# Pooled attention with a rotated token and channel mix: another order of the hand-written table from its 701st piece on

## The chip, the cores and the metric

The kernel runs on one core of a Trainium2 chip. The metric is the device time of one execution in microseconds. TensorE (PE) multiplies matrices; VectorE (DVE), ScalarE (ACT) and GpSimd (POOL) do the elementwise work; SyncE (SP) issues DMAs.

## What is computed

For 8 batches, 8 heads, 576 positions and a head width of 64, in fp32 (q, k and two of the weights are scaled up by 8 in the inputs):

```python
k_p = k.reshape(B, H, Sp, pool, D).mean(axis=3)      # pool = 8, so Sp = 72
v_p = v.reshape(B, H, Sp, pool, D).mean(axis=3)
scores = scale * np.matmul(q, k_p.transpose(0, 1, 3, 2))
attn = softmax(scores)                               # max taken off, sum + 1e-9
x = heads_side_by_side(np.matmul(attn, v_p))         # [8, 576, 512]
theta = x @ w_theta
zr, zi = x * np.cos(theta), x * np.sin(theta)
y = einsum('ts,bsd->btd', w_tok_r, zr) + einsum('ts,bsd->btd', w_tok_i, zi)
u = x + y
out = u + np.maximum(u @ w_ch, 0.0)
```

## The kernel before

The large products are made of three matmuls each: both factors are split into a high part in the matmul's own type (fp32r) and the rest, and high times high, high times low and low times high are added in PSUM. So every elementwise result that feeds TensorE costs a cast and a subtraction more.

The work is cut into streams, one for each step of each batch, and each stream into pieces of one to a few instructions. A stream is a Python generator; each `yield` ends a piece. The letters, with the helper and the lines of its instructions:

- k, v, u: loads of keys and values (L539 kpst, L552 kprst, L542 vpst, L555 vprst). Q: loads of queries, eight DMAs (L634 qsst), and their transpose on DVE (L639 qT). K, V: pooling by halving additions (L191), and the pooled keys' way to PE (L611, L621).
- S, soften: scores (L732), maximum (L774), L792, exponent (L797), sum (L799), reciprocal (L801), normalising (L804), and a DVE transpose into the one buffer G (L819).
- E, turn: eight DMAs of each piece carry G into eraw (L863), of which there is one buffer. X, attend: the products with the pooled values (L885, L894, tiles pv) and the copies into xa and xb, the two halves of x, two buffers each. The copies of batch b + 2 go into the buffers of batch b.
- Y and y: x goes out to memory (L917 xs, L924 hall) and back turned (L932 xt).
- T, rotate: x @ w_theta (casts xe, xh, xl; L947 pt, one PSUM bank), the range reduction (L951 on ACT, L953 on DVE), sine and cosine (L707, L961, L963) and z (L1005, L1007; the last chunk of 64 positions through L994, L1020 and L1022).
- Z, take: the split of z for the mix, zh (L206 on ACT, L208 on DVE or POOL, 128x1152) and zl (L1038 on DVE, L191 on POOL). M, mix: three times nine matmuls (L1053, tiles py), the addition into xa or xb (L1059), and the split of u (uh, and L1066 or L191 ul).
- F, final: three times four matmuls (L1081, tiles pf), `u + max(pf, 0)` (L1086), a DVE transpose into R (L1092, two buffers for all batches but the last) and four DMAs to the output (L1097).

A name like F1.3.0 is batch 1, channel chunk 3, half 0 of the positions (half 0: 256 of them, xa; half 1: 320, xb); T2.4 is batch 2, position chunk 4.

The order is the table SCHEDULE, 2,131 words written out by hand. Each word takes one stream one piece further, and a last letter a, v or g puts the elementwise work of that piece on ACT, DVE or POOL:

```python
for word in SCHEDULE.split():
    name, engine = (word[:-1], word[-1]) if word[-1] in "vga" else (word, None)
    now[0] = engine
    next(streams[name])
```

Instructions stand on each engine in the order in which the table makes them, and each engine works its row in order. All DMAs behind the preparation go through SP's queue but half of those of batch 7's output, which go through ACT's. On POOL an operation on 512 or more columns is cut in two. The next transpose into a buffer of R has to wait until the four DMAs that read it have landed.

Of the kernel before, what the change touches and what calls it, by code (L numbers as in the profile page):

```python
# [1221 lines left out]
```

## Time and profile before

| | |
|---|---|
| median of 3 runs | 589.93 us (589.21, 589.93, 592.08) |
| the profiled execution | 588.76 us, span 587.0 us |
| mean granted clock of TensorE | 0.984 |
| busy: PE, DVE, ACT, POOL | 559.7, 423.4, 307.5, 302.0 us |
| DMA | 70.63 MB, mean 120 GB/s |

The profiled execution's time is the span from the first to the last instruction and 1.8 us around it. Busy times are shares of a span in which the engines work side by side; PE's of 95% says that PE is nearly always at work, and the rest is in single gaps, so one reads what ends each gap and what stands in front of that.

### The profile page before, as it was taken

To read this page: it belongs to the slowest core of one execution; us is meant where nothing else is said; L and a number is where in the kernel's file an instruction comes from. 1 tells how busy PE (TensorE), PEld (TensorE's weight loads), DVE (VectorE), ACT (ScalarE), POOL (GpSimd) and SP (SyncE) were. 2 spreads that over 40 slices of the span, in tenths; PEclk is the share of its full clock that TensorE was granted. 3 is DMA by queue.
4 is the path that set the end of the run, shared out by engine and by line. 5 is a ranking of instruction groups with operands and counts; after the bars stand their busy time and mean duration, and the time that the engine had idled before them with its cause. 6 is when DMAs were issued, how large, how long until landed. Compare 5 with 4: busy or idle time off the path is not lost.

```text
span 587.0 us, 13259 instructions
## 1 busy us (share of the span) xinstructions
PE 559.7 (95%) x4904; PEld 502.4 (86%) x4904; DVE 423.4 (72%) x834; ACT 307.5 (52%) x628; POOL 302.0 (51%) x446
## 2 busy tenths in 40 slices
PE   8779979999999998999999989999999999999996
PEld 7566869888989878989898869899998989989996
DVE  5968997879886876577786868588777876434444
ACT  2867996668635862177527644286422745144100
POOL 1423432348785676664865664483576555352220
PEclk9988979999999998999999999999999999999999
DMA  9985412678375665594555754684445441230215
GB/s 276 273 261 114 121 51 79 114 129 131 80 140 133 151 130 132 120 180 127 108 131 139 152 121 119 132 182 103 94 92 145 116 80 49 55 88 9 41 26 89
DMA packets 191265, 70.63 MB, mean 120 GB/s; under 512 B 149600, under 2 KB 176224, under 8 KB 191200
## 3 DMA queue, kind: packets, MB, share of 16 engines
q1 hardware_dynamic: 186336, 69.18, 53.2%
q10 hardware_dynamic: 4864, 0.59, 0.7%
q8 instruction: 39, 0.64, 0.5%
q14 instruction: 26, 0.21, 0.1%
HBM read 45.15 MB, written 15.73 MB: 104 GB/s over the span
## 4 chain that ended last, share of the span: by engine, by line
PE 72%; DMA 10%; SPq 6%; DVE 5%; ACT 2%; POOL 1%; issue 1%; DVEq 0%; ACTq 0%; POOLq 0%
PE py L1053 36%; PE pt L947 14%; PE pf L1081 11%; SPq L863 2%; PE s L732 2%; DMA z<-in_v_dram 2%; SPq L1097 2%; DMA out_dram<-R 1%; DMA xt<-hall 1%; DMA wraw<-in_moe_w_tok_r_dram 1%; PE pv_av L894 1%; DMA kpst<-in_k_dram 1%; PE pv_av L885 1%; DMA qsst<-in_q_dram 1%; SPq L634 1%
## 5 line engine op out<-in xcount | busy, mean ns | idle before, releaser
L1053 PE MATMUL py<-WTh,zh 128*128 128x256 f32 (+1 forms) x576 | 87.6, 299 | 3.3 <-ACT zh L206 1.3
L1053 PE MATMUL py<-WTl,zh 128*128 128x256 f32 (+1 forms) x576 | 88.4, 298 | 0.0
L1053 PE MATMUL py<-WTh,zl 128*128 128x320 f32 (+1 forms) x576 | 86.8, 297 | 0.0
L1053 PEld LDWEIGHTS py<-WTh,zh 128*128 128x128 f32 x576 | 80.5, 190 | 7.1 <-issue 2.1
L191 POOL TENSOR_TENSOR en<-e_eps,ri 128x256 f32<-128x256 f32 (+3 forms) x74 | 44.3, 616 | 78.6 <-DVE ri L801 48.6
L1053 PEld LDWEIGHTS py<-WTh,zl 128*128 128x128 f32 x576 | 79.6, 189 | 3.0 <-issue 1.3
L1053 PEld LDWEIGHTS py<-WTl,zh 128*128 128x128 f32 x576 | 81.5, 192 | 0.7 <-issue 0.4
L191 POOL TENSOR_TENSOR zl<-z,zh 128x384 fp32r<-128x384 f32 (+1 forms) x68 | 53.4, 817 | 14.1 <-ACT zh L206 9.4
L206 ACT CAST zh<-z 128x1152 fp32r<-128x1152 f32 x22 | 25.3, 1154 | 49.1 <-PE py L1053 41.6
L947 PE MATMUL pt<-th,xh 128*128 128x512 f32 x148 | 42.4, 409 | 3.5 <-ACT xh L206 1.9
L1081 PE MATMUL pf<-uh,chh 128*128 128x256 f32 (+1 forms) x256 | 44.0, 297 | 0.0
L1081 PE MATMUL pf<-uh,chl 128*128 128x256 f32 (+1 forms) x256 | 43.6, 295 | 0.0
L1081 PE MATMUL pf<-ul,chh 128*128 128x256 f32 (+1 forms) x256 | 43.3, 295 | 0.0
L797 ACT ACTIVATE e_eps<-e_eps 128x576 f32<-128x576 f32 (+1 forms) x30 | 20.3, 678 | 43.9 <-DVE e_eps L792 43.9
L947 PE MATMUL pt<-tl,xh 128*128 128x512 f32 x148 | 40.6, 397 | 0.0
L947 PE MATMUL pt<-th,xl 128*128 128x512 f32 x148 | 40.2, 394 | 0.0
L951 ACT ACTIVATE g<-pt,c_magic 128x512 f32<-128x512 f32 x35 | 24.0, 686 | 30.5 <-PE pt L947 23.6
L1081 PEld LDWEIGHTS pf<-uh,chh 128*128 128x128 f32 x256 | 37.5, 188 | 2.5 <-issue 0.5
L1081 PEld LDWEIGHTS pf<-ul,chh 128*128 128x128 f32 x256 | 37.1, 188 | 1.1 <-issue 0.5
L1081 PEld LDWEIGHTS pf<-uh,chl 128*128 128x128 f32 x256 | 37.3, 188 | 0.7
L953 DVE SCALAR_TENSOR_TENSOR g<-g,pt 128x512 f32<-128x512 f32 x35 | 23.8, 681 | 17.2 <-ACT g L951 17.0
L947 PEld LDWEIGHTS pt<-th,xh 128*128 128x128 f32 x148 | 25.9, 192 | 9.3 <-ACT xh L206 2.5
(276 smaller groups left out, 1279.1 us busy)
## 6 DMA issues: line engine op xcount, KB each, us to landing
kpst<-in_k_dram SPq DMA_DIRECT2D x15, 512.0 KB
vpst<-in_v_dram SPq DMA_DIRECT2D x28, 256.0 KB
qsst<-in_q_dram SPq DMA_DIRECT2D x96, 72.0 KB
hall<-xs SPq DMA_DIRECT2D x48, 128.0 KB
xt<-hall SPq DMA_DIRECT2D x12, 512.0 KB
eraw<-G SPq DMA_DIRECT2D x144, 40.0 KB
out_dram<-R SPq DMA_DIRECT2D x112, 40.0 KB
out_dram<-R SPq DMA_DIRECT2D x112, 32.0 KB
```

The lines of the kernel that those rows point to most:

```text
L191: nc.gpsimd.tensor_tensor(out[:, r], a[:, r], b[:, r], op)
L206: nc.scalar.copy(out, src)
L634: queue.dma_start(st[32 * i : 32 * i + 32, S * c : S * c + S].rearrange("p (x a) -> p x a", a=32), q[b, 2 * j + c + 4 * (i // 2)].rearrang ...
L732: nc.tensor.matmul(scs[hh][o : o + 64, SP * c : SP * c + SP], qT[r, c, t0 + o : t0 + o + 64], kpT[r, c, SP * hh : SP * hh + SP], start=Tru ...
L797: nc.scalar.activation(e[:n], e[:n], AF.Exp, scale=scale)
L863: queue.dma_start(Ex[32 * j : 32 * j + 32, 0:m, i], Gx[32 * i : 32 * i + 32, 0:m, j])
L947: nc.tensor.matmul(pt, l[:, c, :], r[:, c, :], start=i == 0, stop=i == 11)
L951: nc.scalar.activation(g, pt, AF.Identity, bias=c_magic)
L953: nc.vector.scalar_tensor_tensor(g, g, MAGIC, pt, ALU.subtract, ALU.subtract)
L1053: nc.tensor.matmul(py[:, :n], l[:, kk, :], r[:, kw, t], start=i == 0, stop=i == 3 * NK - 1)
L1081: nc.tensor.matmul(pv[:, :n], l[:, kk, o], uhl[r][:, kk, t], start=i == 0, stop=i == 11)
L1097: (nc.scalar if b == B - 1 and i % 2 else nc.sync if b == B - 1 else queue).dma_start(out[b, t, ch0 : ch0 + 32].rearrange("(x t) a -> t x ...
```

## The change

All pieces stay, and the first 700 words of the table are the same. From the 701st word on the order differs: a piece stands on average 4.3 places from where it stood, and some loads and poolings up to 110. 120 elementwise pieces get another engine, 44 of them in the mix. Nothing else in the file differs. PE has the same 1,035 rows of the order as before and SP the same 200, in another order; DVE gets nine instructions more, POOL four fewer, ACT 13 fewer, among them six loads of function tables. The table's rows tell a reader little; two lines of its 83:

```diff
@@ -59,83 +59,83 @@
...
-M1.0.1 Y2.0 S3.4 S3.2 T2.1g Z1.2g T2.0 T2.0 T2.0a M1.3.1 M1.0.1g S3.2 M1.0.0 S3.2g E2.2 M1.3.1 S3.2g T2.0 M1.1.1g
...
-F1.3.0 T2.4a T2.4 K4a K4.2g T2.4 F1.0.1 F1.2.0 T2.4 Z2.1a k5.0 E3.0 F1.3.0 Y3.2 K4 Z2.0g F1.1.0 F1.1.0 F1.3.0 K5.0g
...
+M1.0.1 Y2.0 S3.4 S3.2 T2.1g Z1.2g T2.0 T2.0 T2.0a M1.3.1 M1.1.0a M1.3.1 E2.2 M1.0.0 M1.3.1 M1.3.0 T2.1 S3.2 M1.1.0v
...
+k5.0 F1.1.0 T2.4a K4.2g T2.4 T2.4 F1.3.0 T2.4 K5.0g Z2.1v K4a F1.3.0 T3.3a K4 M2.1.0 E3.0 Z2.1v F1.3.0 M2.1.0 M2.1.0
...
```

What that is in instructions, at the places that the prediction speaks of. The listings give line, operation, tiles and shape; a name like R_2_0_3041 is chunk 2, half 0, and a running number. First **SP's queue where the transfers of batch 3's second attention half stand** (eraw_0), before:

```order
L863 DMA eraw_0_3049<-G 32x2x160 x8
L924 DMA hall_2_3019<-xs_2_2914 32x8x128 x2
L863 DMA eraw_0_3049<-G 32x2x160 x8
L542 DMA vpst_1_3132<-in_v_dram 64x2x512 x2
L1097 DMA out_dram<-R_1_0_3070 32x8x32 x4
L1097 DMA out_dram<-R_2_0_3041 32x8x32 x4
L555 DMA vprst_3317<-in_v_dram 64x1x512 x2
L634 DMA qsst_1_3350<-in_q_dram 32x18x32 x8
```

and in the changed kernel:

```order
L863 DMA eraw_0_3079<-G 32x2x160 x16
L542 DMA vpst_1_3166<-in_v_dram 64x2x512 x2
L1097 DMA out_dram<-R_2_0_3156 32x8x32 x4
L555 DMA vprst_3194<-in_v_dram 64x1x512 x2
L1097 DMA out_dram<-R_1_0_3154 32x8x32 x4
L634 DMA qsst_1_3317<-in_q_dram 32x18x32 x8
```

The two pieces of eraw stand side by side, and the load of vprst stands between the two groups of output.

Second, **DVE where the take of batch 2 starts** (the tile z is what the take reads, zh_1 and zl_1 its first results, R_2_0 and R_1_0 results of batch 1), before:

```order
L1020 TENSOR_TENSOR z<-px_4_2994,sn_4_2999 64x512
L1092 STREAM_TRANSPOSE R_2_0_3041<-xa_1380 128x256
L1022 TENSOR_TENSOR z<-px_4_2994,g_4_2981 64x512
L1086 SCALAR_TENSOR_TENSOR xa_1380<-pf_1_0_2988,xa_1380 128x256
L1092 STREAM_TRANSPOSE R_1_0_3070<-xa_1380 128x256
L1038 TENSOR_TENSOR zl_1_3045<-z,zh_1_3044 128x640
L1038 TENSOR_TENSOR zl_1_3045<-z,zh_1_3044 128x512
```

and in the changed kernel:

```order
L1086 SCALAR_TENSOR_TENSOR xa_1380<-pf_1_0_2989,xa_1380 128x256
L1020 TENSOR_TENSOR z<-px_4_3010,sn_4_3030 64x512
L1022 TENSOR_TENSOR z<-px_4_3010,g_4_2987 64x512
L208 CAST zh_1_3054<-z 128x1152
L1038 TENSOR_TENSOR zl_1_3055<-z,zh_1_3054 128x640
L1038 TENSOR_TENSOR zl_1_3055<-z,zh_1_3054 128x512
L1086 SCALAR_TENSOR_TENSOR xa_1380<-pf_3_0_3021,xa_1380 128x256
```

No transpose into R stands between z's parts any more (both stand some ten rows further down), and the cast zh_1, which was on ACT, stands behind z.

Third, **PE at chunk 4 of batch 4's rotation** (pt_4, ahead of the take of batch 4; the pf are final matmuls of batch 3), before:

```order
L947 MATMUL pt_3_4694<-th,xl_3_4421 128x512 x4
L1081 MATMUL pf_0_0_4716<-uh_4206,chh 128x256 x4
L1081 MATMUL pf_1_0_4728<-uh_4206,chh 128x256 x4
L1081 MATMUL pf_1_0_4728<-uh_4206,chl 128x256 x4
L1081 MATMUL pf_1_0_4728<-ul_4207,chh 128x256 x4
L947 MATMUL pt_4_4744<-th,xh_4_4725 128x512 x4
```

and in the changed kernel:

```order
L1081 MATMUL pf_0_0_4678<-uh_4167,chh 128x256 x4
L1081 MATMUL pf_1_0_4695<-uh_4167,chh 128x256 x4
L947 MATMUL pt_3_4709<-th,xh_3_4410 128x512 x4
L947 MATMUL pt_3_4709<-tl,xh_3_4410 128x512 x4
L947 MATMUL pt_3_4709<-th,xl_3_4411 128x512 x4
L1081 MATMUL pf_1_0_4695<-uh_4167,chl 128x256 x4
L1081 MATMUL pf_0_0_4678<-uh_4167,chl 128x256 x4
L1081 MATMUL pf_1_0_4695<-ul_4168,chh 128x256 x4
L947 MATMUL pt_4_4754<-th,xh_4_4732 128x512 x4
```

Two groups of pf matmuls have moved ahead of chunk 3, and five groups instead of four stand ahead of chunk 4.

## Rows read from the trace of the kernel before

**Rows 1.** The windows behind the 700th piece: busy us of each engine, then clock, DMA.

```profile
187.00:352.00 165.00, 157.79 (x1434) 138.93 (x1432) 120.48 (x233) 89.54 (x142) 108.78 (x160) 0.99 0.63 137
225.00:250.00 25.00, 23.95 (x185) 22.71 (x185) 14.27 (x28) 4.11 (x8) 15.61 (x22) 0.93 0.57 127
226.04:230.50 4.46, 4.46 (x24) 4.46 (x25) 2.09 (x4) 0.18 (x1) 0.98 (x3) 0.62 0.57 172
352.00:455.00 103.00, 101.89 (x942) 93.37 (x943) 79.54 (x153) 45.94 (x74) 60.14 (x87) 1.00 0.58 124
455.00:581.30 126.30, 126.30 (x974) 118.86 (x973) 69.22 (x143) 42.88 (x62) 48.28 (x70) 1.00 0.31 61
```

**Rows 2.** TensorE's waits from 185 to 587 us: us in total, times, longest us.

```profile
PE pt L947 <- ACT xh L206: 1.9, 3, 0.8
PE pt L947 <- DVE g L953: 1.6, 1, 1.6
PE py L1053 <- ACT zh L206: 1.3, 1, 1.3
PE py L1053 <- DVE xb L1086: 1.1, 1, 1.1
...
PE py L1053 <- DVE zh L208: 0.4, 1, 0.4
```

**Rows 3.** The chain of waits at 222 to 228 us: start, us, what.

```profile
221.94 1.73 DMA out_dram<-R
...
224.84 1.16 ACT zh L206
```

**Rows 4.** The same chain view at 341 to 361 us.

```profile
341.79 1.90 DMA eraw<-G
...
346.08 3.23 DMA out_dram<-R
...
352.20 3.01 PE pt L947 x12
```

**Rows 5.** SP's timeline, its DMA issues: start, us, engine, line, operation, count.

```profile
185.22 1.33 SPq L542 DMA_DIRECT2D vpst<-in_v_dram  x2
...
243.41 1.32 SPq L555 DMA_DIRECT2D vprst<-in_v_dram  x2
...
268.21 13.55 SPq L863 DMA_DIRECT2D eraw<-G  x16
...
337.32 5.06 SPq L863 DMA_DIRECT2D eraw<-G  x8
342.49 4.05 SPq L1097 DMA_DIRECT2D out_dram<-R  x8
```

**Rows 6.** SP's waits from 185 to 352 us, first and last of 22 groups.

```profile
SPq L1097 <- DVE ri L801: 1.7, 2, 1.5
...
SPq L924 <- DVE z L1007: 0.2, 1, 0.2
```

**Rows 7.** Groups by line and shape over the whole span: busy us, mean ns of one, idle before.

```profile
L707 ACT ACT_TABLE_LOAD x22 | 28.2, 1283 | 1.9 <-DVE g L953 1.5
...
L206 ACT CAST zh<-z 128x1152 fp32r<-128x1152 f32 x22 | 25.3, 1154 | 49.1 <-PE py L1053 41.6 <-POOL z L191 3.1 <-DVE z L1022 1.8
...
L208 DVE CAST zh<-z 128x1152 fp32r<-128x1152 f32 x4 | 3.0, 756 | 0.2
```

**Rows 8.** The chain of waits at 240 to 252 us: start, us, what.

```profile
242.92 1.65 DMA out_dram<-R
...
245.40 0.72 DVE ul L1066 x2
246.12 1.34 DVE zl L1038 x2
...
250.84 1.20 PE pt L947 x4
```

**Rows 9.** VectorE's timeline from 262 to 270 us, one row.

```profile
266.17 0.84 DVE L819 STREAM_TRANSPOSE G<-en 128x640 f32<-128x640 f32 x1
```

More of the change, by code (lines that the diff above doesn't have):

```diff
@@ L136 @@
-F7.2.1 M7.2.0 F6.2.0 F7.3.1 M7.2.0 M7.2.0v F7.2.1 F7.3.1 F7.3.1 M7.3.0g F7.2.0 M7.0.0g M7.2.0v F7.2.0 F7.3.1 F7.3.1
-F7.2.0 F7.2.0 F7.3.0 F7.3.0 F7.3.0 F7.1.0 F7.2.0 F7.2.1g F7.3.1g F7.1.0 F7.1.0 F7.3.0 F7.3.0 F7.1.0 F7.0.0 F7.0.0
-F7.0.0 F7.2.0g F7.1.0 F7.3.0g F7.0.0 F7.1.0a F7.0.0 F7.0.0a
+M1.0.1 Y2.0 S3.4 S3.2 T2.1g Z1.2g T2.0 T2.0 T2.0a M1.3.1 M1.1.0a M1.3.1 E2.2 M1.0.0 M1.3.1 M1.3.0 T2.1 S3.2 M1.1.0v
+y2.0 M1.3.1 S3.2g S3.2g M1.0.1a M1.3.0 S3.3 M1.1.1g T2.0 E2.2 S3.3 v3.1 M1.0.1v T2.0v F0.0.1 S3.3 S3.2 F0.0.1 S3.3g
@@ new lines @@
+M1.3.0 S3.3v M1.3.0 M1.3.0a V3.1g S3.4 S3.4 T2.1 M1.3.1a M1.2.1 M1.2.1 F0.2.1 S3.3 S3.4 X2.2 S3.4g Y2.2 S3.4g M1.2.1
+u3 X2.2a Y2.2 Y2.2 F0.1.1 X2.2a M1.2.1 X2.2a M1.2.0 T2.0v T2.4a S3.4 T2.1 T2.1 T2.2v M1.3.1v S3.1 S3.0 M1.2.0 T2.1
+k4.2 M1.2.1g T2.1 M1.2.0 M1.2.1v T2.2g F1.1.1 T2.1a T2.1 F1.1.1 T2.3a M1.3.0v T2.1v T2.2 M1.2.0 F0.2.1 F1.1.1 F1.3.1
+T2.2 M1.2.0a S3.0 k4.0 Y2.2 F1.3.1 S3.0 T2.1g F1.1.1 F1.3.1 S3.0 T2.2 M1.0.0a F1.2.1 T2.3g V3g S3.0g Y2.2 S3.0g F1.3.1
+F1.3.1 F1.1.1 F1.0.1 E3.2 S3.1 F1.0.1 T2.2 S3.1 y2.2 F1.0.1 T2.2 E3.2 F1.2.1 F1.0.1 F1.2.1 S3.1 K4.0g T2.2 S3.0 T2.2a
@@ new lines @@
+M2.0.1 T2.4 M2.0.0 v4.2 M2.0.1 M2.0.1 Z2.2v M2.0.0 X3.0 M2.0.1 V4.2g F1.1.0 M2.0.1v M2.0.0 M2.1.1v Z2.3a M2.1.0g V4.1v
+Z2.3v M2.0.0 F1.0.0 Y3.0 F1.3.0 M2.2.1 X3.0v X3.0a X3.0a M2.2.1 K4v Y3.0 M2.2.1 M2.0.0a Q4.1 T3.1a M2.2.1 V4g Y3.0
+M2.3.0 M2.0.0v M2.3.0 k5.2 T3.1v M2.2.1v T3.1 Q4.1 T3.1 Y3.0 M2.2.0 T3.1 S4.0 T3.0a S4.0 Y3.0 T3.1 T3.1 v4.0 S4.1
+M2.2.0 S4.0 M2.2.1g T3.1 S4.0 F1.0.0 S4.0v K5.2g M2.0.1g M2.2.0 M2.3.0 T3.1a T3.0g y3.0 M2.2.0 S4.0g M2.2.0a T3.0 T3.0
+S4.1 T3.1 S4.1 S4.0 T3.1v M2.3.0 V4.0g M2.3.0a M2.3.1 T3.0 T3.1v M2.2.0g S4.1 T3.2a M2.3.1 F1.3.0 T3.0 S4.1g M2.3.1
@@ new lines @@
+F2.0.0 M2.3.0g S4.1v T3.0 T3.0 y3.2 Q5.0 S4.1 F2.0.0 T3.0a k5.1 T3.0 M2.3.1 T3.3 T3.3 T3.0v T3.0v F2.0.0 T3.3 v5.2
+K5.1g S4.3 S4.2 T3.2v F2.0.0 F2.2.0 F2.2.0 F2.2.0 T3.3 T3.3 F2.2.0 T3.2 E4.0 M2.3.1a T3.3 T3.3a T3.2 E4.0 T3.3 S4.2
+F2.2.0 S4.2 T3.2 T3.3g M2.3.1g F2.2.1 T3.3v F2.1.1 T3.2 S4.2 F2.1.1 F2.2.1 F2.2.1 T3.2 T3.2 F2.1.1 S4.2g F2.0.0 K5
+F2.2.1 F2.3.1 F2.2.0 T3.2a S4.2g F2.1.1 F2.0.1 S4.3 T3.2 F2.3.1 F2.3.1 S4.2 T3.2g v5.1 F2.0.1 F2.0.1 F2.3.1 F2.0.0
+T3.2g Z3.0a F2.0.1 F2.2.1 S4.4 F2.2.1 S4.3 M3.0.0 F2.1.0 Q5.0 u4 K5a Z3.0g M3.0.0 S4.3 F2.1.0 F2.1.0 S4.3g F2.1.0
@@ new lines @@
+F2.3.0 M3.0.0 F2.3.0 S4.3g S4.4 Q5.1 F2.1.0 F2.3.0 S4.4 X4.0 Z3.1a S4.3 F2.1.0 F2.3.0 K5 V5.1g Z3.1g M3.0.0 S4.4
+F2.3.0 Y4.0 X4.0v Y4.0 v5.0 S4.4g M3.0.1 M3.0.1 X4.0v Y4.0 X4.0a M3.0.1 S4.4g K5a Q5.1 S4.4 F2.3.0 M3.1.1 S5.2 Y4.0
+Z3.2a S5.2 T4.0a F2.0.1 T4.1g S5.2 M3.1.1 M3.0.1 V5.2g Y4.0 E4.2 S5.2 T4.1v T4.0g T4.0 M3.1.1 T4.0 T4.0 S5.3 M3.1.0
+T4.0 y4.0 M3.1.0 Z3.3a M3.1.1 M3.1.1a F2.3.1 V5.0g Z3.2v M3.1.0 M3.0.1v S5.2v S5.2g S5.4 M3.0.0a M3.1.0 S5.3 M3.2.1
+M3.2.1 E4.2 S5.3 T4.0 Z3.3g M3.2.1 v6.1 T4.1 M3.0.1g S5.3 M3.3.0 S5.2 T4.0 S5.3g S5.3g S5.4 T4.0a T4.0 M3.3.0 M3.3.0
@@ new lines @@
+F2.0.1 F2.1.1 T4.0g S5.3 X4.2 M3.2.1 M3.3.0 Y4.2 M3.3.1 S5.4 M3.2.0 Y4.2 Y4.2 M3.1.0a S5.4 Q6.0 k6.2 M3.2.1a X4.2v
+T4.0g V6.1g S5.4g X4.2a F2.1.1 T4.1 X4.2v T4.1 T4.1 M3.1.1v Y4.2 S5.4v T4.3v T4.3g M3.2.1g T4.2a S5.4 F2.3.1 M3.2.0
+Y4.2 T4.2g S5.0 S5.0 M3.3.0g M3.2.0 T4.1 M3.2.0 M3.3.1 k6.0 M3.3.1 M3.3.1 K6.2g S5.0 S5.1 M3.3.1v M3.1.0v M3.2.0a T4.1
+F3.1.1 M3.3.0v M3.3.1v F3.3.1 F3.3.1 F3.1.1 V5v F3.1.1 T4.1a S5.0 F3.1.1 F3.3.1 S5.0v T4.2 T4.1 F3.1.1 S5.0g F3.3.1
+S5.1 E5.2 S5.1 y4.2 T4.1g T4.2 T4.2 F3.2.1 M3.2.0g F3.3.1 F3.2.1 T4.1g F3.2.1 F3.0.1 S5.1 u5 E5.2 T4.2 F3.2.1 F3.0.1
@@ new lines @@
+S6.1 S6.2 T5.0a M4.2.1 T5.3 F4.1.0 T5.2a F4.1.0 F4.1.0 T5.0 T5.0v T5.3 T5.0v M4.1.1g T5.2v F4.1.0 T5.3 M4.3.1 T5.3
+K7.0g k7.1 T5.3 F3.3.0 M4.3.1 M4.3.1 F4.1.0 S6.2 T5.3 M4.3.1 T5.3v E6.0 S6.2 T5.3 K7.1g T5.2 T5.2 K7.2g M4.2.1a S6.2
+T5.3v T5.3v T5.2 M4.3.1a M4.2.1v F4.0.0 F4.0.0 F4.0.0 F4.0.0 F4.3.1 T5.2 T5.2 M4.3.1g S6.2v T5.2 F4.3.1 T5.2a T5.2
+S6.2g F4.1.0 F4.3.1 E6.0 F4.2.1 S6.3 S6.4 F4.3.1 F4.3.1 S6.3 F4.2.1 F4.2.1 T5.2g F4.2.1 F4.0.0 Q7.0 S6.3 F4.3.0 F4.3.1
+F4.3.0 F4.3.0 T5.2g Z5.1g F4.1.1 F4.1.1 F4.1.1 Z5.0a F4.3.0 F4.2.0 F4.0.0 S6.2 Z5.0g v7.1 M5.0.0 F4.1.1 M5.0.0 M5.0.0
@@ new lines @@
+Q7.1 u6 S6.3 M5.0.1 S6.3g F4.2.1 S6.3g M5.0.0 K7 M5.0.1 K7a S6.4 Z5.1v M5.0.1 F4.2.0 K7 X6.0 F4.2.1 Z5.2g M5.1.0 S6.3
+S6.4 S6.4 S6.4g S6.4v M5.1.0 F4.3.0 X6.0a X6.0a M5.1.0 S6.4 M5.0.1 F4.3.0 M5.1.1 Y6.0 M5.1.0 Q7.1 Y6.0 Y6.0 M5.1.1 K7v
+F4.0.1 F4.0.1 Z5.2g V7.1g F4.0.1 X6.0a M5.1.1 F4.0.1 Z5.3a E6.2 F4.0.1 M5.1.1 S7.2 S7.2 E6.2 Y6.0 S7.3 M5.2.1 M5.2.1
+S7.2 Z5.3v M5.0.1a M5.2.1 F4.1.1 M5.3.1 Y6.0 F4.0.1 M5.3.1 S7.2 S7.2g S7.2v S7.3 M5.2.1 M5.1.1a X6.2 M5.3.1 M5.3.0
+S7.2 S7.3 X6.2a S7.3 X6.2v M5.1.1g X6.2a M5.3.0 Y6.2 Y6.2 Y6.2 S7.4 y6.0 M5.0.0g M5.0.1g T6.3a S7.3g T6.3v M5.3.0
@@ new lines @@
+M5.3.1 S7.3g T6.3 S7.4 Y6.2 M5.1.0g M5.3.1g S7.4 M5.3.0 S7.3 T6.3 M5.2.1g Y6.2 M5.3.1g M5.2.1g S7.4 T6.3 v7.2 F5.2.1
+F4.1.1 M5.3.0v S7.4v F5.2.1 u7 F5.2.1 S7.0 V7.2g T6.2g M5.2.0 S7.4v T6.3 T6.3 S7.4 T6.2g M5.2.0 S7.0 T6.3 F5.2.1 T6.3v
+S7.0 M5.3.0v T6.2 F5.1.1 T6.2 T6.1v y6.2 T6.2 T6.3 T6.3v T6.0a T6.3v E7.2 M5.2.0 F5.2.1 M5.2.0 T6.2 T6.2 T6.0g E7.2
+F5.1.1 F5.1.1 F5.0.1 T6.2 S7.0 F5.0.1 T6.0 T6.0 V7g F5.1.1 F5.1.1 T6.2a F5.1.1 T6.2 S7.0v T6.2v T6.0 T6.2v F5.3.1
+F5.3.1 T6.4v T6.1v F5.3.1 M5.2.0a T6.0 M5.1.0v X7.2 T6.0 F5.0.1 F5.3.1 T6.0 F5.3.1 F5.2.1 T6.0a M5.0.0g Y7.2 T6.1
@@ new lines @@
+M5.2.0g F5.0.1 T6.0 T6.1 F5.2.0 F5.0.1 X7.2a T6.1 T6.0g Y7.2 F5.2.0 X7.2a T6.0g X7.2v F5.1.0 Y7.2 F5.1.0 T6.1 Y7.2
+S7.1 F5.0.1 T6.4g F5.2.0 T6.1 T6.4a F5.1.0 T6.4v T6.1 T6.1v Y7.2 T6.4 F5.3.1 F5.1.0 T6.1 F5.2.0 T6.4 T6.4 F5.3.0
+F5.0.0 F5.3.0 T7.2g S7.0g T6.1g T6.1v F5.0.0 S7.1 T7.3a T6.4 T6.4 T7.2v T6.4 T7.3g T7.2 T6.4 y7.2 T6.4v F5.0.0 T6.4
+T7.2 F5.3.0 T7.2 T6.4 T6.4 Z6.1v F5.0.0 T6.4 S7.1 F5.3.0 F5.1.0 Z6.1g S7.1 Z6.0a M6.1.0 M6.1.0 M6.1.1 M6.1.0 T6.4 S7.0
+M6.1.0 T7.2 Z6.0g S7.1g M6.1.1 S7.1g T7.2 M6.1.1 Z6.3a S7.1 Z6.3g M6.0.1 M6.1.1 M6.0.1 F5.1.0 M6.0.1 M6.0.0 M6.0.0
@@ new lines @@
+T7.1 F6.3.0 T7.0v F6.3.0 T7.0v F6.3.0 F6.1.1 F5.2.0 T7.1 F6.1.1 T7.1 F6.3.0 F6.3.0 F6.1.1 F6.1.0 T7.1 F6.1.0 F6.3.1
+F6.1.0 F6.1.0 F6.1.0 F6.3.1 F6.3.1 F6.3.1 F6.0.0 F6.0.0 F6.2.0 T7.1a T7.1 F6.0.0 T7.1g T7.1g Z7.0v F6.3.0 F6.2.0
+F6.1.0 F6.0.0 F6.2.0 M7.0.0 Z7.0v M7.0.0 F6.2.0 F6.0.1 M7.0.1 M7.0.1 Z7.1a Z7.1v M7.0.0 M7.0.0 M7.0.1 M7.0.1 M7.1.1
+M7.1.1 M7.1.1 M7.0.1v M7.1.1 M7.1.0 F6.0.0 M7.0.0v M7.1.0 Z7.2g Z7.2g Z7.3v M7.1.1v M7.1.0 M7.2.1 Z7.3g M7.2.1 M7.2.1
+M7.1.0 M7.3.1 M7.3.1 M7.0.1g M7.3.1 F6.0.1 M7.2.1 F6.0.0 F6.1.1 M7.3.1 M7.2.1v M7.3.0 M7.3.0 M7.3.1v M7.3.0 M7.2.1v
@@ new lines @@
+M7.1.1v F6.2.1 F7.1.1 F6.1.1 F6.3.1 F7.1.1 M7.3.0 F6.2.1 M7.3.1g M7.3.0a F7.1.1 F7.1.1 M7.1.0v F7.1.1 F7.0.1 F7.0.1
+F7.0.1 M7.3.0g M7.2.0 F7.0.1 F7.0.1 F7.1.1g M7.1.0g M7.0.0g F7.2.1 F6.2.0 F7.2.1 F7.2.1 F7.0.1g M7.2.0 F7.2.1 M7.2.0
+F7.3.1 M7.2.0 M7.2.0g F7.3.1 F7.2.1 F7.3.1 F6.3.1 F7.2.0 F6.2.0 F7.2.0 M7.2.0g F7.2.1v F7.2.0 F7.3.1 F7.3.1 F7.3.0
+F7.3.0 F7.3.1a F7.3.0 F7.2.0 F7.1.0 F7.2.0 F7.3.0 F7.1.0 F7.1.0 F7.3.0 F7.0.0 F7.1.0 F7.2.0a F7.1.0 F7.3.0v F7.1.0g
+F7.0.0 F7.0.0 F7.0.0 F7.0.0 F7.0.0a
```

91 lines of the change are left out of this document (19 added, 72 removed).

## The prediction

> **What bounds the kernel now.** I read the windows first, then TensorE's waits, then the DMA queue's own timeline and waits, then the chain of waits at the two places where TensorE stood longest. The order of the two kernels is the same up to the 700th piece, at about 185 us, so only what lies behind counts. There the windows [rows 1] show three stretches. From 187 to 352 us PE is busy 157.79 of 165.00 us, so it stands for 7.2 us, and from 226.04 to 230.50 it is busy throughout but at a granted clock of 0.62, a mix of its two levels 2.4 and 1.2 GHz: at full clock that work would have taken 4.46 x 0.62 = 2.8 us, so 1.7 us are lost. From 352 to 455 us it stands for 1.1 us, from 455 to 581.3 us not at all, and the last 5.7 us are the tail behind the last matmul. All that any order of the rest can win from PE's stalls is therefore 7.2 + 1.7 + 1.1 = 10.0 us, which would put the profiled run's 588.76 us at 578.8.
>
> PE's waits [rows 2] say on whom: a cast of x (xh) on ACT, a range reduction (g) on DVE, the casts of z (zh) on ACT and DVE, an addition into xb on DVE. None is a slow engine. The chain behind the first of the two long ones [rows 3] goes back to a transfer: an out-going DMA of an earlier batch lands at 223.67, only then may DVE transpose the next result into its buffer R; the z that the take of batch 2 needs stands behind that transpose on DVE, the cast (zh, at 224.84) behind z on ACT, and the first mix matmul (226.04) behind the cast. The chain behind the other [rows 4] has the same form with a queue in front: SP's last of eight out-going issues is done at 346.08, it lands 3.23 us later, then come an R on DVE, ACT's copy of the next attention result, ACT's and DVE's g, and the rotation of chunk 4 of batch 4 (pt4_4) starts at 352.20.
>
> So the second bound is **the SP queue**. Its timeline [rows 5] reads as a belt without gaps: the eight transfers of eraw take 5.06 us to issue at 337.32, the eight out-going ones 4.05 at 342.49. From 185.22 us to the end of that last row, 346.54, the order lists 253 issues on SP, in the kernel before and in the changed one, of the same kinds in the same numbers: 161.3 us / 253 = 0.64 us each. SP's own waits for somebody else in that stretch [rows 6] are 22 groups, from 1.7 us down to 0.2 each, 11.6 us in all. Whatever PE wins, a gate that opens with the 253rd issue comes earlier only as far as those 11.6 us shrink.
>
> Here a rule speaks against this reading. The Trainium skill, page "DMA: Bandwidth & Descriptors", section "Issuing engines are not separate DMA queues", says that the time a sequencer takes to initiate a DMA "is usually small relative to the DMA itself"; by it the queue could not hold the gains, and rival A below would be the forecast. The trace does not agree: the issues of one eraw piece take 5.06 us and the last of them lands 1.90 us after it [rows 4, 5].
>
> **The change part by part.** The pieces are the same, so PE's rows and SP's issues are the same sets. PE's own order hardly differs: the rows ahead of the gates are the same but for one group of four pf matmuls ahead of pt4_4. At the pace of the stretch behind 455 us, 974 matmuls in 126.30 us [rows 1], that is 4 x 0.13 = 0.5 us.
>
> *Fewer table loads.* ACT loses six ACT_TABLE_LOADs of 1,283 ns [rows 7], 7.7 us. I cost this at nothing: ACT is busy 89.54 of the 165 us [rows 1], and none of PE's waits goes back to a load. Without that cover it could be at most the ACT part of each chain.
>
> *The take of batch 2 (226 us).* The R transposes are moved behind the take, one cast of z goes from ACT (1,154 ns) to DVE (756 ns) [rows 7], and two pairs of zl from POOL to DVE. The wait of 1.30 us and the low clock behind it can go: at most 1.3 + 1.7 = 3.0 us here. At least nothing.
>
> *The rotation of batch 3 (250.84 us).* PE then reaches pt3_1 up to 3.0 us earlier, but pt3_1 waits for a chain from the SP queue [rows 8]: an out-going DMA, the last of its eight issued at 242.9, lands at 244.57; behind it come DVE's R, more work on DVE, ACT's copy and ACT's cast xh, 6.27 us down to pt3_1. In the changed order four of those eight issues stand behind vprst's two, which take 1.32 us [rows 5], so the landing comes at 245.9; DVE's queue behind R loses ul and zl (0.72 + 1.34), and I hold its lost vprst additions against the two small copies that it gains. That gives 245.9 + 6.27 - 2.06 = 250.1, 0.7 us earlier than before. So of the 3.0 us some 0.7 are left here, and the rest becomes a longer wait at pt3_1.
>
> *From there to 352 us.* What is won (0.7, and 1.1 at 286 us if R's wait there goes) runs into pt4_4. Its chain [rows 4] starts with the 253rd issue, at the same time in both kernels if SP waits as long as before. So it opens at 352.2 again, PE waits longer, and the gain is given back: nothing. The extra pf group fills 0.5 us of that wait, but it is then missing behind pt4_4, as cover for the chain to the first mix matmul of batch 4, where PE already waited 0.4 us for zh [rows 2] and would wait 0.9. Zero net. Bounds: a gain of all stalls up to there (8.9 us) if SP's waits vanish with PE's, a loss by rival B.
>
> *Behind 352 us.* The last of the waits for xh, 0.42 us at 379 us, is behind an R that waits for a DMA; the four issues in front of it come about 1 us earlier in the changed queue, so it goes: -0.4. From there PE was never idle, so engine letters changed there can only cost: a cast of z is 0.4 us longer on ACT than on DVE [rows 7], at the head of a take. An order in which the mix matmuls of batch 7 stand behind three more groups of final matmuls hides that. Zero, at worst 0.4 us in each of three takes.
>
> *Sum.* 588.76 - 0.4 = 588.4 for the profiled run. The median of the three runs shown is 589.93, 1.17 us above that run, so the forecast is 588.4 + 1.17 = **589.5 us**: no change that can be told. Its own range is 587.0 to 591.5, from the gate coming 2 us earlier or later.
>
> **The rivals.** A: *the queue does not hold the gains.* SP's waits are for the same late pieces that PE waits for; if they shrink with PE's by some 4 of 11.6 us, the gate moves along. Then 3.0 us at 226, 1.1 at 286 and 0.4 at 379 go: 588.76 - 4.5 + 1.17 = 585.4. For it speaks that SP's waits are many and end on DVE, ACT and POOL [rows 6]; against it that the longest single wait in them is 1.6 us and that no one of them explains a delay of SP as a whole. With every stall gone it is 578.8 + 1.17 = 580.0.
>
> B: *slower, DVE too late for the queue.* DVE takes over two pairs of zl and a zh, 2 x 1.34 + 0.756 = 3.4 us [rows 7, 8], and the three additions that pool one chunk of values, none longer than that zh of more than twice their width: up to 5.7 us between 225 and 250, where it is busy 14.27 of 25.00 us [rows 1]. If the scores of batch 4 thereby come late, so does their G: it is written at 266.17 to 267.01 [rows 9], and SP comes to read it at 268.21 for 16 issues [rows 5]: 1.2 us of slack. Beyond that SP stands, and the later gate moves with it one for one. The gate has no slack, since PE already waits there, so 1.2 us late costs nothing, 4.8 us late 3.6 us: 588.76 + 3.6 + 1.17 = 593.5. Against it speaks DVE's idle 10.7 us, which hold the 5.7.
>
> C: *the change has no effect in its own places:* the wait at 226 us stays as it is, since z (L1022) is behind another late step. Then it is 589.9, inside the forecast's own range.
>
> **How the numbers follow.** Forecast 0.46, C 0.07, both within 0.5% (2.95 us, about what a measurement of this kernel can tell from no change); A 0.27 and its far end with all stalls gone 0.03, both faster; B 0.17, slower. So faster 0.30, same 0.53, slower 0.17. The range from 584.2 to 593.4 holds the forecast, C, A with about 1 us below it, and B up to some 3.5 us of cost; what it leaves out is A's far end and the worse half of B, some 0.12, and at most 0.08 more for what no case here names.
>
> **What would show it.** Right: the wait at 226 us is gone and the clock stays at its full level behind it; pt3_1 still starts at 250 to 251 us and its wait has grown to about 3 us; SP issues the eight out-going DMAs from 342 to 347 us; pt4_4 starts at 351.5 to 353 us with a wait above 1.6 us; the rows behind it are the old ones less 0.4 us. Rival A shows as the same SP rows 3 us or more earlier, B as a wait of SP for G near 268 us and pt4_4 behind 354 us. The prediction is wrong if pt4_4 starts before 350 us, or if idle time appears behind 455 us, where PE had none.

## The result, and the profile after

The changed kernel takes 584.00 us, the median of 14 runs (581.85 to 589.37), and the kernel before, timed beside it, 589.11 us, the median of 14 (586.16 to 592.08). The ratio is 0.9919, with a 95% interval from 0.9894 to 0.9944: faster by 0.8%, more than the 0.5% that the prediction called a difference. The forecast's likeliest case, no change at 589.5 us, did not come true; what came is near rival A (585.4). The ratio puts the changed kernel at 0.9919 x 589.93 = 585.2 us against the runs that the forecast was set against. That is inside its range of 584.2 to 593.4 us, which reaches so far down because it holds rival A, a case that the forecast gave 0.27.

The profiled execution took 583.87 us, its span is 582.1 us. The windows of the changed kernel (columns as in [rows 1]):

```profile
187.00:352.00 165.00, 159.39 (x1457) 140.43 (x1457) 125.04 (x243) 86.28 (x135) 105.30 (x160) 1.00 0.64 138
225.00:250.00 25.00, 25.00 (x218) 23.06 (x220) 18.64 (x34) 4.93 (x8) 9.32 (x16) 1.00 0.58 135
352.00:455.00 103.00, 102.33 (x982) 93.86 (x981) 81.84 (x151) 49.03 (x78) 60.37 (x88) 1.00 0.59 127
455.00:576.40 121.40, 120.23 (x906) 113.29 (x904) 68.05 (x140) 32.16 (x50) 47.91 (x65) 1.00 0.28 55
```

From 225 to 250 us PE now never stands (23.95 of 25.00 us before), and over the whole stretch from 187 to 352 us the granted clock is 1.00 (0.99 before, with 0.62 from 226.04 to 230.50). In the last two rows there is little to win or lose: 0.7 us of standing still instead of 1.1, and 1.2 us behind 455 us where there was none.

PE's waits of the changed kernel, the four largest (from 185 to 582 us, columns as in [rows 2]):

```profile
PE pv_s L885 <- issue: 1.8, 2, 1.6
PE pt L947 <- POOL xh L208: 1.2, 1, 1.2
PE py L1053 <- DVE zh L208: 0.8, 2, 0.6
PE py L1053 <- DVE xb L1059: 0.6, 1, 0.6
```

Of the five waits of [rows 2] those for xh on ACT and zh are down to 0.2 us and 0.8 us in all; the wait of 1.2 us is pt4_4's, now for a cast on POOL, and the 1.6 us are at a product of the attention.

SP's timeline of the changed kernel, the places that answer to [rows 5], and the two outputs that stand around vprst:

```profile
183.65 1.34 SPq L542 DMA_DIRECT2D vpst<-in_v_dram  x2
...
236.21 2.02 SPq L1097 DMA_DIRECT2D out_dram<-R  x4
238.28 1.32 SPq L555 DMA_DIRECT2D vprst<-in_v_dram  x2
239.64 1.92 SPq L1097 DMA_DIRECT2D out_dram<-R  x4
...
265.06 10.98 SPq L863 DMA_DIRECT2D eraw<-G  x16
...
337.65 4.04 SPq L1097 DMA_DIRECT2D out_dram<-R  x8
```

The first of the 253 issues starts at 183.65 us (185.22 before) and the last ends at 337.65 + 4.04 = 341.69 (346.54). So SP's row takes 158.0 us, and took 161.3. The 16 issues of eraw take 10.98 us at 265.06, and took 13.55. The 1.57 us by which the row starts earlier are not the change's: up to there both kernels are the same instructions, and in the twelve traces of kernels that share them, here and below, the row starts anywhere from 183.03 to 186.56 us.

The chain of waits of the changed kernel in front of pt4_4 (start, us, what), which answers to [rows 4]:

```profile
341.24 3.00 DMA out_dram<-R
...
344.67 0.52 DVE R L1092
...
345.28 0.82 DVE xb L208
...
346.77 0.62 POOL xh L208
...
347.48 3.04 PE pt L947 x12
```

The form is the old one, with a cast at its end where the range reduction was: SP's last out-going issue, its landing, R, a copy of the next attention result, a cast, pt4_4. SP still opens this gate; it opens it at 347.48 instead of 352.20.

Laid end to end, the difference of the two spans, 4.9 us, is 1.6 us from the common beginning (chance), 3.3 us from SP's row, -0.1 from the way between the row's end and pt4_4 (5.7 and 5.8 us), and 0.2 us from everything behind pt4_4 (234.8 and 234.6). What the prediction held for stiff, the row, has become shorter. The ratio of all runs stands for 4.8 us (0.0081 x 589.1); without the chance at the beginning the two traces show 3.4 of them, and the rest of the gain is not located.

Counted from the start of SP's row, the changed kernel comes to the first mix matmul of batch 2 1.25 us earlier (at 223.22 instead of 226.04) and to pt3_1, the gate at 250 us, 3.7 us earlier (at 245.61 instead of 250.84); between the two lie the 1.7 us of low clock and the 0.8 us that PE waited at pt3_1 before. What the forecast did not expect is that this lead is kept at pt3_1. VectorE of the changed kernel there:

```profile
239.63 1.15 DVE L521 TENSOR_TENSOR vpst<-vpst 128x512 f32<-128x512 f32 x2 [2.69 <-issue]
...
241.02 1.42 DVE L1038 TENSOR_TENSOR zl<-z,zh 128x640 fp32r<-128x640 f32 x2
...
242.69 0.43 DVE L1092 STREAM_TRANSPOSE R<-xa 128x256 f32<-128x256 f32 x1
...
243.38 0.40 DVE L1092 STREAM_TRANSPOSE R<-xa 128x256 f32<-128x256 f32 x1
...
245.27 0.76 DVE L917 STREAM_TRANSPOSE xs<-pv_s 128x256 f32<-128x256 f32 x2
```

and ScalarE:

```profile
243.87 0.37 ACT L206 COPY xa<-pv_px 128x256 f32<-128x256 f32 x1 [5.93 <-DVE R L1092]
244.14 0.59 ACT L206 COPY xa<-pv_s 128x512 f32<-128x512 f32 x1
...
244.93 0.63 ACT L206 CAST xh<-xa 128x512 fp32r<-128x512 f32 x1
```

and TensorE, at the take of batch 2 and at pt3_1:

```profile
223.22 1.32 PE L1053 MATMUL py<-WTh,zh 128*128 128x256 f32 x9 [0.64 <-DVE zh L208]
...
245.61 1.20 PE L947 MATMUL pt<-th,xh 128*128 128x512 f32 x4
```

DVE's pooling of values (L521, L526) and the zl of the last take stand ahead of R now, and DVE does not stand in front of R for a landing. Of the three copies of the attention's results (xa) DVE makes one (pv_av) and ACT two (pv_px, pv_s), directly behind R and ahead of DVE's transposes xs of the same tiles: pv_s is copied at 244.14 and transposed at 245.27. In [rows 8] R was followed by 4.1 us of DVE work, the transposes of pv_s last, and only then by ACT's last copy; in the trace's records that copy waits for a semaphore which DVE counts up behind these transposes. From R's end at 243.78 to pt3_1 it is 1.8 us, and pt3_1 at 245.61 waits for nothing.

### The profile page after: what moved, and what is told of

The parts are those of the page before. It is cut to its first block, busy times and chain, and to the rows that moved or that the text cites. A ratio compares the mean times of both kernels' runs of the same rounds, so it can differ in the third digit from the quotient of the medians.

```text
span 582.1 us, 13236 instructions
## 1 busy us (share of the span) xinstructions
PE 555.7 (95%) x4904; PEld 498.6 (86%) x4904; DVE 429.5 (74%) x843; ACT 297.3 (51%) x615; POOL 299.3 (51%) x442
## 4 chain that ended last, share of the span: by engine, by line
PE 77%; DMA 6%; SPq 5%; DVE 4%; ACT 3%; POOL 2%; issue 1%; DVEq 0%; ACTq 0%; POOLq 0%
PE py L1053 37%; PE pf L1081 15%; PE pt L947 14%; SPq L863 4%; PE s L732 2%; DMA kpst<-in_k_dram 2%; PE pv_av L894 1%; PE pv_av L885 1%; DMA z<-in_v_dram 1%; DMA wraw<-in_moe_w_tok_r_dram 1%; DMA qsst<-in_q_dram 1%; PE pv_px L885 1%; DMA out_dram<-R 1%; PE s_av L732 1%; SPq L1097 1%
## 5 line engine op out<-in xcount | busy, mean ns | idle before, releaser
L191 POOL TENSOR_TENSOR en<-e_eps,ri 128x256 f32<-128x256 f32 (+3 forms) x79 | 46.0, 604 | 81.5 <-DVE ri L801 54.6
L1053 PEld LDWEIGHTS py<-WTl,zh 128*128 128x128 f32 x576 | 80.2, 189 | 1.0 <-issue 0.4
L191 POOL TENSOR_TENSOR zl<-z,zh 128x256 fp32r<-128x256 f32 (+1 forms) x60 | 46.4, 806 | 18.0 <-ACT zh L206 11.4
L191 POOL TENSOR_TENSOR kpst<-kpst 128x256 f32<-128x256 f32 x30 | 24.3, 823 | 17.0 <-DMA kpst<-in_k_dram 16.2
```

Of the source, the lines that this page charges most:

```text
L191: nc.gpsimd.tensor_tensor(out[:, r], a[:, r], b[:, r], op)
L1053: nc.tensor.matmul(py[:, :n], l[:, kk, :], r[:, kw, t], start=i == 0, stop=i == 3 * NK - 1)
```

## The experiments

The theory tested first: SP's row of 253 issues is the second bound, a gate opens as much earlier as SP's pauses shrink (the belt theory). Its rival: the wait and the low clock at 226 us are the cost, PE keeps what it wins there, and SP only follows (the chain theory). In kernels whose table was written anew, line numbers are one lower than in the kernel before.

**Three parts of the order.** Hybrids of the two tables, cut where their first words are nearly the same sets.

```diff
-the words of before
+x1: the changed order to the 980th word, then the old order of the rest
+x2: the old order to the 980th word, the changed one to the 1340th, the old one
+x3: the old order to the 1340th word, then the changed one
```

> The changed order up to the 980th piece (about 250 us, the start of batch 3's rotation), the old order of what is left behind it. Belt theory: SP's queue is nearly full from 185 to 346 us, 253 issues, and a gate opens as much earlier as SP's pauses shrink (17.7 us before, 14.5 us after); up to 240 us SP had won 2.0 us, the two pauses of 1.7 and 0.9 us at 272 to 275 us come back with the old order, so some 2 us faster than before (587). Chain theory: what counts is the wait and the low clock at 226 us that are gone, SP only follows; PE stood 3.8 us earlier at pt3_1 (prefix taken off) and keeps that: 585.3.

Measured: 582.13 us, ratio 0.9885 (0.9853 to 0.9916). The first part alone brings the whole gain, more than either theory allowed.

> The old order up to the 980th piece, the changed one to the 1340th (250 to 352 us), the old one behind. Belt theory: SP's pauses at 272 to 275 us go (2.5 us), and pt4_4 comes 1.3 to 2.5 us earlier: 586.6 to 587.8. Chain theory: nothing to win there, since the 3.8 us were made before: within 0.6 us of before.

Measured: 584.06 us, ratio 0.9910 (0.9879 to 0.9941), more than either theory allowed. Its profiled run took 586.25 us, 2.2 above its median, and shows SP's row at 161.4 us, as long as before; so what shortened the other runs no trace here shows. Each of the first two parts thus has about the whole gain by itself, and they do not add up.

> The old order up to the 1340th piece (about 352 us), the changed one behind. Both theories: only what PE wins behind pt4_4, 1.4 us in the two traces, 0.4 at pt5_1 and the rest at 445 to 490 us, less what the tail gives back (1.2 us there): 588 to 589. More than 2 us faster would say that the gain is made in the second half, and speak against both.

Measured: 588.71 us, ratio 0.9998 (0.9976 to 1.0019). Nothing is won behind 352 us.

**The letters and the order apart.**

```diff
@@ x4: the changed order, each piece with its letter of before @@
-K5.0g Z2.1v K4a
+K5.0g Z2.1a K4a
...
@@ x5: the old order, each piece with its letter of the changed table @@
-T2.4 Z2.1a k5.0
+T2.4 Z2.1v k5.0
...
```

> The changed order throughout, with the engine letters of the kernel before for each piece. Belt theory: SP's row and its place between the others are those of the changed kernel, so most of the gain stays, 3 to 5 us faster than before. Chain theory: the cast of z at 223 us is on ACT again (1.15 instead of 0.76 us) and zl on POOL, so the mix matmuls of batch 2 wait again, and half of the gain is lost: 2 us faster.

Measured: 587.65 us, ratio 0.9987 (0.9963 to 1.0010), no gain where both theories had one.

> The order of before throughout, with the engine letters of the changed kernel for each piece. If the gain is the letters' own, 4 us faster than before (584 to 585); if letters and order only work together (the cast of z moved to DVE behind the R that waits for a DMA), within 1.5 us of before.

Measured: 591.67 us, ratio 1.0044 (1.0010 to 1.0078), some 2.6 us slower, outside what was expected. The order without the letters is worth nothing that can be told, the letters without the order cost; the gain is of both together. The window of x4 behind the take of batch 2 (columns as in [rows 1]):

```profile
226.00:232.00 6.00, 4.96 (x30) 4.87 (x31) 2.36 (x4) 0.93 (x4) 1.43 (x2) 0.72 0.72 179
```

PE stands 1.0 us in it and runs at a clock of 0.72, with the cast zh on ACT and zl on POOL again.

**Sixteen issues more.**

```diff
+        if b == 2 and hf == 1:
+            h = n // 2
+            for i in range(8):
+                ch0, e = P * c + 32 * (i // 2), h * (i % 2)
+                nc.sync.dma_start(
...
```

> The kernel before, with the output of batch 2's half 1 sent in eight DMAs of half the size for each chunk instead of four: 16 issues more on SP between 270 and 300 us, the same bytes and the same data. Belt theory (SP's row of issues sets when pt4_4 at 352 us may start, and PE already waits there): 16 issues of 0.35 to 0.5 us more, so pt4_4 and the end come 5 to 8 us later, 593 to 596. Theory that SP only follows PE and the elementwise engines: within 1 us of before.

Measured: 595.48 us, ratio 1.0112 (1.0068 to 1.0156), about 7 us more. The belt theory had it right, the theory that SP only follows did not. SP's timeline of this kernel, one of the four outputs that became eight issues, and the last issues of the row:

```profile
290.37 3.92 SPq L1098 DMA_DIRECT2D out_dram<-R  x8
...
353.18 4.09 SPq L1106 DMA_DIRECT2D out_dram<-R  x8
```

The row ends at 357.27 us instead of 346.54; it starts at 186.56 and takes 170.7 us, 9.4 longer; at 3.92 us for eight, the 16 issues more are 7.8 us of that. And a wait for eraw's landing has come in on PE (its waits from 185 to 600 us):

```profile
PE pv_av L884 <- DMA eraw<-G: 3.5, 1, 3.5
```

**Twenty issues fewer.**

```diff
-        queue = nc.sync
         for c in range(2):
+            queue = nc.scalar if c else nc.sync
```

> The kernel before, with four of the eight DMAs of each load of queries issued on ACT's queue: SP loses 20 of its 253 issues from 185 to 346 us (some 12 us), ACT gets them (0.5 to 0.6 us each, between its other work). Belt theory: PE's waits behind SP shrink, 2 to 5 us faster than before (583 to 586). Theory that SP only follows: no gain, and up to 3 us slower since ACT's casts wait behind the issues.

Measured: 600.01 us, ratio 1.0184 (1.0142 to 1.0226), far slower than either theory allowed.

> The changed kernel with the same four of eight DMAs of each load of queries on ACT's queue. Belt theory: the changed kernel is held by the same queue (pt4_4 waits 1.2 us for a chain that starts with SP's 253rd issue), so it gains too, to 580 to 583. Theory that SP only follows: 584 or slower.

Measured: 588.69 us, ratio 1.0008 (0.9978 to 1.0039) to the kernel before, by the two ratios some 5 us slower than the changed kernel. Neither got faster. Fewer issues alone do not make the row shorter: with 233 the row still takes 158.5 us in the changed kernel and 166.6 in the old one. SP now waits instead for the very loads that ACT issues late (SP's waits in the old kernel with 20 fewer, from 187 to 354 us: us in total, times, longest us):

```profile
SPq L1096 <- DMA qsst<-in_q_dram: 7.6, 4, 4.2
SPq L923 <- DMA qsst<-in_q_dram: 5.1, 2, 2.7
```

These are out-going transfers that need nothing of a load of queries. In the trace's records SP's and ACT's issues share the eight semaphores that count landings, and an issue of SP waits there until the load that ACT issued on the same semaphore has landed: the longest of these waits ends at 271.71 us with a load that ACT issued only at 269.02. So as a test of relief the experiment is spoiled. The changed kernel's row also starts 3.7 us later; the loads of the earlier batches were moved as well. What it shows is that SP's row is held from two sides, by its issues and by the landings that they wait for.

**One transfer moved.** In the old trace SP pauses 1.7 and 0.9 us in the issues of eraw at 268.21 [rows 5], and goes on at 274.01 and 275.46, where a load of kpst and one of xt, 512 KB each, have landed (SP's waits of the kernel before from 185 to 352 us, columns as above):

```profile
SPq L863 <- DMA kpst<-in_k_dram: 1.6, 1, 1.6
SPq L863 <- DMA xt<-hall: 0.9, 1, 0.9
```

These are waits that the program asks for. In the trace's records SP's issues take eight semaphores in turn, and each waits until the issue eight places ahead of it, the last one on its semaphore, has landed; so it is with all 253 issues of the row from the ninth on. The two issues that pause are the seventh and the eighth of eraw, eight places behind kpst and xt; the last counts of these two loads come at 273.99 and 275.45 us, 0.02 us ahead of the issues. In the changed order this xt stands far ahead.

```diff
-Q5.0 ... F1.3.0 ... y3.2
+y3.2 Q5.0 ... F1.3.0 ...
```

> The kernel before with one piece moved: the load xt<-hall of batch 3's second half (512 KB) stands 26 words earlier, behind the other xt<-hall, and no longer between kpst's 512 KB and eraw. Belt theory with its cause: SP's pauses of 1.7 and 0.9 us in eraw's issues at 272 to 275 us end with the landings of kpst and of this xt, so they shrink to one of at most 1 us or go; SP's 253 issues take 158.5 to 159.5 us instead of 161.3, and the end comes 1.5 to 2.8 us earlier (586 to 587). If the pauses have another cause (G late, chance), no change.

Measured: 587.91 us, ratio 0.9992 (0.9966 to 1.0019).

> The changed kernel with the same load put back directly ahead of eraw, behind kpst and vprst. Belt theory with its cause: the pauses come back (2 to 2.8 us), SP's row takes 160 to 161 us and the kernel 586 to 587. If the changed kernel's gain has its place at 226 us, no change: 584.

Measured: 584.23 us, ratio 0.9925 (0.9896 to 0.9955) to the kernel before: as fast as the changed kernel.

> The changed order up to the 980th piece, the old one behind, and the load xt<-hall moved ahead as well. If both shorten SP's row by themselves: 2 to 2.8 us faster than that hybrid (582.1), 579.5 to 580. If PE has meanwhile become the bound in that stretch, 581.5 to 582.5.

Measured: 582.99 us, ratio 0.9922 (0.9897 to 0.9948), no faster than the hybrid x1. SP's timelines at this place, first of the old kernel with the load early:

```profile
256.33 0.92 SPq L931 DMA_DIRECT2D xt<-hall  x2
...
268.76 0.40 SPq L538 DMA_DIRECT2D kpst<-in_k_dram  x1
269.28 10.88 SPq L862 DMA_DIRECT2D eraw<-G  x16
```

then of the changed kernel with the load late:

```profile
264.48 0.45 SPq L931 DMA_DIRECT2D xt<-hall  x1
265.03 12.57 SPq L862 DMA_DIRECT2D eraw<-G  x16
```

The 16 issues take 10.9 us without the load in front (13.55 before) and 12.6 with it (10.98 in the changed kernel). So the pauses have the cause that was named, and still taking them away is worth nothing: the row of the old kernel with the load early takes 162.1 us as a whole. It was wrong to read a cause of the gain from the one place where two traces differ most.

**The take of batch 2 alone.**

```diff
-the words of before
+the changed order from the 880th to the 930th word, the old order before and behind
```

> The changed order of the 880th to the 930th piece alone (the take of batch 2: R's transposes behind it, the cast zh on DVE, two zl on DVE), the old order before and behind. Chain theory: the wait of 1.3 us and the low clock at 226 us go and stay gone: 3 us faster (585.5). Belt theory: PE comes 3 us earlier to pt3_1 at 250 us, and gives back what SP's row does not follow: 0 to 1 us faster.

Measured: 586.91 us, ratio 0.9993 (0.9971 to 1.0015). The chain theory falls here, in that PE does not keep what it wins at 226 us. All of PE's waits of this kernel from 222 to 262 us:

```profile
224.65 1.33 PE L1052 MATMUL py<-WTh,zh 128*128 128x256 f32 x9 [1.22 <-DVE zh L207]
...
252.31 2.07 PE L946 MATMUL pt<-th,xh 128*128 128x512 f32 x4 [5.20 <-ACT xh L205]
```

and VectorE ahead of the second:

```profile
246.50 0.45 DVE L1091 STREAM_TRANSPOSE R<-xa 128x256 f32<-128x256 f32 x1 [2.55 <-DMA out_dram<-R]
...
250.16 0.77 DVE L916 STREAM_TRANSPOSE xs<-pv_s 128x256 f32<-128x256 f32 x2
```

The take starts 1.4 us earlier than in the trace of before, 0.7 of it from the common beginning, and the clock behind it stays full (1.00 from 226 to 232 us). But the output now stands behind vprst, R waits until 246.50, and the work behind R on DVE is the old one, 4 us long: pt3_1 waits 5.20 us, and behind that wait the clock is low as well (0.66 from 248 to 258 us). What the forecast said of the whole change, that the gain at 226 us is given back at pt3_1, is what these 50 pieces alone do.

**All traces together.** For each traced kernel: the time from the first of SP's issues at 183 to 187 us to pt3_1, the length of SP's row to the last of R3_1_1's output, from there to pt4_4, from pt4_4 to the span's end, PE's granted clock from 187 to 352 us, and the median of its runs.

| kernel | to pt3_1 | SP's row | to pt4_4 | rest | clock | median us |
|---|---|---|---|---|---|---|
| before | 65.6 | 161.3 | 5.7 | 234.8 | 0.99 | 589.11, 588.41, 588.52, 587.96 |
| x3, new from 352 us | 65.9 | 161.4 | 6.0 | 235.3 | 0.98 | 588.71 |
| x5, new letters | 65.2 | 163.0 | 6.1 | 236.6 | 0.97 | 591.67 |
| xt early | 66.4 | 162.1 | 5.6 | 234.8 | 0.99 | 587.91 |
| take of batch 2 | 67.8 | 163.1 | 4.2 | 235.0 | 0.98 | 586.91 |
| x4, new order | 67.0 | 160.5 | 6.0 | 236.2 | 0.99 | 587.65 |
| x2, new 250 to 352 us | 66.6 | 161.4 | 5.3 | 234.2 | 0.98 | 584.06 |
| 16 issues more | 65.9 | 170.7 | 5.3 | 233.8 | 0.99 | 595.48 |
| before, 20 fewer | 68.0 | 166.6 | 5.4 | 239.6 | 0.98 | 600.01 |
| changed | 62.0 | 158.0 | 5.8 | 234.6 | 1.00 | 584.00 |
| changed, xt late | 62.4 | 158.1 | 6.1 | 234.5 | 1.00 | 584.23 |
| x1, new to 250 us | 62.5 | 159.0 | 4.2 | 234.1 | 1.00 | 582.13 |
| x1, xt early | 63.2 | 160.3 | 4.2 | 233.9 | 1.00 | 582.99 |
| changed, 20 fewer | 63.7 | 158.5 | 5.3 | 234.3 | 1.00 | 588.69 |

Three things stand in it. In all 14 kernels pt4_4 follows the end of SP's row by 4.2 to 6.1 us, and what comes behind pt4_4 takes 233.8 to 236.6 us in all but one: most of the difference between kernels is in SP's row. That is not yet a cause: PE waits at pt4_4 in ten of the traces, and in four it does not. In two of these, x1 with xt early and the 16 issues more, PE has waited for eraw's landing shortly before (1.1 and 3.5 us), so SP holds it by another gate; in the take of batch 2 it waits for neither. In x1, the fastest kernel, the chain in front of pt4_4 is PE's own work from 324 us on, and pt4_4 starts without a wait:

```profile
349.10 1.17 PE L946 MATMUL pt<-th,xh 128*128 128x512 f32 x4
```

The five kernels that have the changed order and letters up to 250 us are the five that reach pt3_1 after 62.0 to 63.7 us (the others after 65.2 to 68.0), keep the full clock throughout, and have a row of 158.0 to 160.3 us (the others 160.5 and more; the changed kernel with 20 fewer is a row of 233 issues). The gap between the two groups of rows is 0.2 us, with one trace of each kernel; at pt3_1 and in the clock the groups are clearly apart. And x2 stands outside: with the old beginning and, in its trace, the old row, its runs are as fast as the changed kernel's. That stays open.

## Why the prediction was right or wrong

*The bound.* Right for the two kernels that the forecast compares: in both traces PE waits at pt4_4 for a chain from the end of SP's row, and adding 16 issues made the kernel 7 us slower. It is not so in every trace: in x1 the row does not hold pt4_4. The Trainium skill, page "DMA: Bandwidth & Descriptors", section "Issuing engines are not separate DMA queues", says that initiating a DMA is usually small relative to the DMA itself. The prediction set the eight issues of a piece against one landing; for a single out-going transfer the sentence fits these rows, 4.05 us for eight issues [rows 5] and 1.65 to 3.23 us from an issue to its landing [rows 4, 8]. It does not carry over to a row of issues: 16 more without a byte more cost 9.4 us of the traced row.

*The take of batch 2.* Right: the wait of 1.30 us is 0.64 us in the changed trace, and the low clock behind it is gone. Right too that by itself this wins nothing, because it is given back at pt3_1, as the experiment with these pieces alone shows.

*The rotation of batch 3.* Wrong, and here the forecast failed first. It put pt3_1 at 250.1 us, 0.7 us earlier than before; it started at 245.61, or 3.7 us earlier against the start of SP's row (62.0 instead of 65.6 us). Two terms were off. The landing was put at 245.9 us; the last four out-going issues end at 241.56, and in the trace's records they have landed at 243.22. That is 2.7 us before the forecast, 1.6 of them the common beginning, the rest SP's waits up to there. The other term, "6.27 - 2.06 us" from the landing to pt3_1, came to 2.4 instead of 4.2 us. It took the DVE work behind R as one queue that ACT's last copy has to wait out. In the changed order that copy stands ahead of DVE's transposes of the same tile, and from R's end to pt3_1 it is 1.8 us. The forecast compared DVE's rows and did not read ACT's and DVE's order against each other. No run changes this order alone, so its share is read from two traces and not tested.

*"At the same time in both kernels if SP waits as long as before."* Wrong by 3.3 us: the row took 158.0 us. SP's waits from 185 to 352 us [rows 6] fell from 11.6 to 8.3 us, but 2.0 of the 8.3 stand behind the changed row's end. In the rows themselves they fell from 11.3 to 6.3 us, and rival A had asked for 4. So the step "it opens at 352.2 again", the one that made the gain nothing, failed by 4.7 us, 1.6 of them chance. The row did not become shorter with the take alone (163.1 us), whose gain ends at pt3_1. A lead at pt3_1 and a short row go together in the five kernels; that the one makes the other is likely and not shown. By which of SP's waits it would do so was not isolated: in x1's row of 159.0 us the two pauses in eraw stand as before.

*Behind 352 us.* Right in size: 0.4 us was the forecast, 0.2 us the traces, and the changed order from there on alone is worth nothing (0.9998). In detail it was not: idle time of 1.2 us did appear behind 455 us, where the prediction had none.

*The rivals.* A came true in what it said of SP's waits, by another door than the one it named. That its 585.4 us meets the measured 585.2 so closely is luck in part, since the two traces show 3.4 us where it added up 4.5. B's late G did not come: SP reads G at 265.06 us without a pause. Both signs that were to show the forecast wrong came true: pt4_4 before 350 us (347.48, and 349.05 without the chance at the beginning), and idle time behind 455 us. Of the signs for it the first came, the shorter wait at 226 us and the full clock behind it, and nearly the last, rows behind pt4_4 that take 0.2 us less; pt3_1, SP's eight out-going issues and pt4_4 all stood elsewhere.

## What to carry to other kernels

Where an in-order queue and an in-order engine take turns in holding a gate, price both against each other: read in which order two engines stand at the same tile, not only what each has to do. A gain in front of such a gate is kept only if the gate opens earlier too, so an edit and the pieces behind it are to be tried together; here the order and the engines were each worth nothing alone. Before a queue is called full, look up what its pauses wait for: here they were landings eight issues back. And the place where two traces differ most need not be where the time is: the pause that they showed most plainly was worth nothing on the chip.

## What the runs showed of the hardware

An issue on SP takes 0.46 us for an out-going transfer and 0.59 us for one of eraw (chain rows at 340.73 us in the changed kernel and at 339.88 us in the old one), and they stand one behind another. With eight semaphores in turn a queue is never more than eight transfers ahead of its landings: the issues of eraw stood at 272.34 and 274.59 us until 512 KB loads eight places ahead of them had landed. Taking one load away shortened these 16 issues by 2.7 us and the whole row by nothing.

A low granted clock, 2.4 and 1.2 GHz mixed, stands in each of the nine traces without the changed order and letters up to 250 us: in six behind a wait of PE at 226 us (0.61 to 0.88 in a window of 4.5 or 6 us), in three behind the wait at pt3_1 instead (0.62 to 0.66 in one of 9 or 10 us). None of the five traces with it has one there. The trace of x5 has two more, from 283 to 289 us and from 325 to 331 us (0.72 in each). The waits ahead of the nine were from 1.1 to 5.2 us long, and length alone does not tell: 1.10 us at 224 us in x2 was not followed by a low clock, 1.14 in x5 was, and the 1.6 us at 352.20 in the kernel before were not (1.00 from 352.20 to 358.20).
